# An FNet mixing and SoLU kernel: w_out loaded whole behind x, the first weight product moved into the first transform, copies of turned u shared between two engines, the second pair's sums two steps later

## Chip, cores and metric

The kernel runs on one core of a Trainium2 chip. The metric is device time in microseconds (us) of one execution; each kernel was run several times and medians are given. Engine names are those of the profile: PE multiplies matrices (PEld is its weight load), DVE is the vector engine, ACT the scalar engine, POOL is GpSimd, SP issues most transfers. A profile covers one execution; its span is 1.8 us shorter than the time that the same execution reports (1212.1 against 1213.89 before).

## The reference, cut to what matters

```python
x: (8, 3136, 256)
X = fft(fft(x, axis=1), axis=2).real            # FNet mixing, 3136 = 49 * 64
h = X.reshape(25088, 256) @ w_in                 # w_in (256, 1024)
e = exp(h - max(h)); sm = e / (sum(e) + 1e-9)
solu = h * sm
ln = (solu - mean(solu)) / sqrt(var(solu) + 1e-6) * g_ln
out = ln @ w_out                                 # w_out (1024, 256)
```

w_in and w_out arrive as 64-bit floats. The kernel computes in 32 bits, so it narrows them on DVE, mostly with integer operations, a piece of 512 columns at a time ("narrowing", about 4.5 us a piece).

## The kernel before

The batches go in four pairs. For each pair a first transform (matmuls with the table F, eight chunks) makes z and stores it to memory (`zd`); a gather (`turn`) reads it back turned, as g; a second transform (table T) gives q. Then come units, 25 for a pair and 100 in all; unit 0 of a pair has one sign, the others two. For a unit PE multiplies q with the folded weight Wi (`up`), DVE makes `even`, `join` (with the maximum), and later `product`; ACT does the exponentials and squares; the result u is turned and, four units later, multiplied with Wo (`down`). While a pair's units run, the next pair is loaded, summed with its mirror image, folded and transformed. The first four units' u are turned on PE (`turn_whole`), all later ones by DVE and transfers.

The parts that the change touches, with cuts marked by `# ...`:

```python
def fold_features(o, i):
    # ... two tensor_tensor on DVE
    nc.scalar.copy(o[:, :, 0:129:128], i[:, :, 0:129:128])     # the edge columns

def turn_whole(t):
    # ...
    for s in t.signs:
        for half in range(2):
            # ... four PE turns into a PSUM tile ps
            nc.scalar.copy(uT[:, half * n : (half + 1) * n, :, s], ps)

def centre(self):      # Wo -= its column mean
    # ... 8 matmuls with ones into cs
    nc.scalar.mul(out=wbar, in_=cs, mul=1.0 / FF)
    nc.vector.tensor_tensor(out=Wo, in0=Wo, in1=wbar..., op=ALU.subtract)

def ahead(pr, step):          # the next pair: chunk c summed at step 2+2c, folded one later
    c, r = divmod(step - 2, 2)
    # ...
        if r == 0: add_mirror(pr, c, nc.gpsimd)
        else:      fold(pr, c) # ...

# the opening
weights.piece_in(0)
load(first, 0)
nc.sync.dma_start(out=F, in_=f_tab)
for c in range(1, 4):
    weights.piece_in(c)
    load(first, c, rooms.get(c))
for c in range(4, 6):
    load(first, c, rooms[c])
weights.load_tables()
# ...
for c in range(NC):
    if c < 4:
        weights.narrow_in(c)
    add_mirror(first, c, nc.vector)
    fold(first, c)
    # ...
    elif c == 3:
        weights.place_out()
        weights.load_out(0)
        # ...
    for s in range(CH // 2):
        transform1(first, c * CH // 2 + s)
weights.load_out(1)
turn(first, 0)
weights.place_table()
for h in range(3):
    weights.product_in(h)
for i in range(KF * D // NW):
    weights.narrow_out(i)

# a step of the main loop
even(cur, up(cur, 0)); odd = up(cur, 1)
# ... second transform of the unit after next; its q copied by ACT
turn_whole(prv)            # only units 0 to 3
join(cur, odd)
expo(cur)
ahead_pe(ahd, cur.k1)      # first-transform matmuls of the next pair
ps_o = [down(old, s) for s in old.signs]
product(cur, s)            # each sign
square(cur, s)             # each sign
# ...
stats(cur)
if i == 0:
    weights.centre()
```

Of the kernel before, what the change touches and what calls it, by code (L numbers as in the profile page):

```python
# [20 lines left out]
NK = N1 // 2 + 1  # L21
NH = N2 // 2
PR = 2 * N1
ZR = 4 * NK
CH = 4
NC = NH // CH

KG = 5
# [6 lines left out]
def kernel(  # L35
# [19 lines left out]
    nc = tc.nc  # L55
# [59 lines left out]
            nc.sync.dma_start(out=x0, in_=x_pn[r, 0:1, :])  # L115
        pr.raw[c] = (xa, xb, x0)

    def fold_features(o, i):
        up, down = i[:, :, 1:128], i[:, :, 255:128:-1]
        nc.vector.tensor_tensor(out=o[:, :, 1:128], in0=up, in1=down, op=ALU.add)  # L120
        nc.vector.tensor_tensor(out=o[:, :, 129:256], in0=up, in1=down, op=ALU.subtract)
        nc.scalar.copy(o[:, :, 0:129:128], i[:, :, 0:129:128])  # L122

    def add_mirror(pr, c, engine):

# [6 lines left out]
    def fold(pr, c):  # L132

        xa, _, x0 = pr.raw.pop(c)
        y = xpool.tile([PR, CH, D], FP32, tag="y", name="y")
        fold_features(y, xa)
        pr.y[c] = y
        if c == NC - 1:
            pr.y0 = xpool.tile([PR, 1, D], FP32, tag="y0", name="y0", bufs=1)
            fold_features(pr.y0, x0)  # L140

    def transform1(pr, s):

# [28 lines left out]
    def turn(pr, i):  # L172

        pr.g[i] = gpool.tile([P, KG, D], FP32, tag="g", name="g")
        for j in range(4):
            k = j * NK + i * KG
            nc.gpsimd.dma_start(out=pr.g[i][j * NH : (j + 1) * NH, :, :],  # L177
                                in_=pr.zd[k : k + KG, :, :].rearrange("k n d -> n k d"))
# [58 lines left out]
    def expo(t):  # L237
        t.esum = small.tile([P, 2], FP32, tag="esum", name="esum")
        for s in t.signs:
            t.u[s] = fpool.tile([P, FF], FP32, tag="u", name="u", bufs=2)  # L240
            nc.scalar.activation(out=t.u[s], in_=t.h[s], func=ACT.Exp, bias=t.neg[:, s : s + 1],  # L241
                                 accum_out=t.esum[:, s : s + 1])
# [45 lines left out]
    def turn_whole(t):  # L288

        uT = t.batch.uT[:, t.w].rearrange("p c i (n s) -> p c (i n) s", s=2)  # L290
        n = KF // 2
        for s in t.signs:
            for half in range(2):
                ps = ps_m.tile([P, n, P], FP32, tag="m", name="ps_t")
                for c in range(n):
                    f = half * n + c
                    nc.tensor.matmul(ps[:, c, :], t.u[s][:, f * P : (f + 1) * P], ident, is_transpose=True,
                                     start=(c == 0), stop=(c == n - 1), skip_group_check=True)
                nc.scalar.copy(uT[:, half * n : (half + 1) * n, :, s], ps)

    def move_blocks(batch, units, engines=(nc.sync,)):

# [152 lines left out]



    def ahead(pr, step):

        c, r = divmod(step - 2, 2)  # L460
        if step == 0:
            load(pr, 0)
            load(pr, 1)
        elif 0 <= c < NC:
            if r == 0:
                add_mirror(pr, c, nc.gpsimd)
            else:
                fold(pr, c)
                if c + 2 < NC:
                    load(pr, c + 2)  # L470

    def ahead_pe(pr, step):

        if 0 <= step - 4 < NH // 2:
            transform1(pr, step - 4)
        elif step - 4 >= NH // 2:
            turn(pr, step - 4 - NH // 2)

    with tc.manual_schedule():
        pairs = [Pair(p) for p in range(NP)]  # L480
# [4 lines left out]
        rooms = {}  # L485
# [2 lines left out]
            room = room[0:PR].rearrange("p w c i m -> p (w c i m)").rearrange("p (a n) -> p a n", a=4)  # L488
            rooms[c], rooms[c + 1] = [room[:, i] for i in (0, 1)], [room[:, i] for i in (2, 3)]
        weights.load_in()  # L490
        weights.piece_in(0)
        load(first, 0)
        nc.sync.dma_start(out=F, in_=f_tab)
        for c in range(1, 4):
            weights.piece_in(c)
            load(first, c, rooms.get(c))
        for c in range(4, 6):
            load(first, c, rooms[c])
        weights.load_tables()
        nc.vector.memset(ones, 1.0)  # L500
        nc.vector.memset(neg_half, -0.5)
        bits(top_bit, neg_half[:, 0:1].bitcast(I32), 31, ALU.logical_shift_right, 31, ALU.logical_shift_left)
        nc.vector.memset(T, 0.0)
        for c in range(NC):
            if c < 4:
                weights.narrow_in(c)
            add_mirror(first, c, nc.vector)
            fold(first, c)
            if c + 6 < NC:
                load(first, c + 6)  # L510
            if c == 1:
                weights.load_table()
            elif c == 3:
                weights.place_out()
                weights.load_out(0)
                weights.mid()
                weights.scale_out()
            for s in range(CH // 2):
                transform1(first, c * CH // 2 + s)
        weights.load_out(1)  # L520
        turn(first, 0)
        weights.place_table()
        for h in range(3):
            weights.product_in(h)
        for i in range(KF * D // NW):
            weights.narrow_out(i)
# [7 lines left out]
        for i in range(len(units) + lag):  # L534
# [18 lines left out]
                turn_whole(prv)  # L553
            if cur:
                join(cur, odd)
                expo(cur)
            if ahd:
                ahead_pe(ahd, cur.k1)
# [2 lines left out]
            if cur:  # L561
                for s in cur.signs:
                    product(cur, s)
                for s in cur.signs:
                    square(cur, s)
                    if i >= whole:
                        turn_blocks(cur, s)
            if old:
                scale(old, 0, ps_o[0])
            if cur:  # L570
# [2 lines left out]
                elif cur.w and i >= whole:  # L573
                    move_blocks(batch, slice(0, 2))
                stats(cur)
            if i == 0:
                weights.centre()
            if 0 < i + 1 < NK // KG:
                turn(first, i + 1)
            if ahd:  # L580
# [80 lines left out]
```

## Time and profile before

| what | before | where it is read |
|---|---|---|
| time, median | 1215.85 us (1213.6 to 1216.08, 3 runs) | runs |
| time of the profiled execution | 1213.89 us | runs |
| span | 1212.1 us | page |
| second transform starts | 72.25 us | PE in order of time |
| even of unit 0 starts | 78.91 us | DVE in order of time |
| PE's last wait ends | 118.50 us | PE's waits and its order of time |
| span less that moment | 1093.6 us | worked out |

PE is busy 96% of the span, and after 118.50 us it never waits again. The prediction below shows the lines that this reading rests on. What it calls "the lock" is the 2.3 us by which DVE's product of unit 3 is longer beside POOL's sum: 3.51 us, against 1.22 without it. In a profile line xN counts instructions: a matmul of the program that is not a turn stands there as two (the 8 of `centre` as x16).

### The profile page before, as it was taken

How to read it: one execution, taken by the hardware profiler on the slowest of the kernel's cores; microseconds unless marked ns; L12 is line 12 of the kernel's file. 1: busy time of each engine (PE TensorE's matmuls, PEld its weight loads, DVE VectorE, ACT ScalarE, POOL GpSimd, SP SyncE). 2: the span in 40 equal slices, each digit the busy share in tenths (PEclk: the TensorE clock that was granted, in tenths of full speed). 3: DMA queues.
4: the chain of work that ended last, by engine and by line, in shares of the span. 5: the costliest groups of instructions: out<-in, count | busy, mean ns of one | idle time of the engine just before them, and what ended most of it. 6: DMA issues, size and time to landing. Idle time of an engine off the chain costs nothing. (4 is left out here: it accounts for less than half of the span.)

```text
span 1212.1 us, 15808 instructions
## 1 busy us (share of the span) xinstructions
PE 1166.4 (96%) x4720; PEld 881.5 (73%) x4720; DVE 903.2 (75%) x1240; ACT 644.8 (53%) x1301; POOL 544.0 (45%) x966
## 2 busy tenths in 40 slices
PE   2787999999999999999999999999999999999998
PEld 1444777777777777777777777777777777777787
DVE  7857877777777877777777887777686787778770
ACT  1237655655555565565554555556555555555551
POOL 3027545444554555543453555544463333333333
PEclk9998999999999999999999999999999999999999
DMA  9733688976999888867899889887899587775765
GB/s 237 209 99 104 130 173 159 171 146 127 179 177 171 155 187 167 165 146 136 163 186 189 147 174 168 168 160 141 155 167 163 103 134 124 124 136 102 135 112 114
DMA packets 457382, 184.98 MB, mean 153 GB/s; under 512 B 425510, under 2 KB 439086, under 8 KB 457296
## 3 DMA queue, kind: packets, MB, share of 16 engines
q1 hardware_dynamic: 443216, 144.89, 68.1%
q0 software_dynamic: 14080, 39.08, 12.5%
q8 instruction: 38, 0.62, 0.2%
q14 instruction: 48, 0.39, 0.1%
HBM read 44.37 MB, written 38.80 MB: 69 GB/s over the span
## 5 line engine op out<-in xcount | busy, mean ns | idle before, releaser
L314 PE MATMUL ps_o<-Wo,uT 128*128 128x256 f32 x3136 | 693.2, 379 | 0.0
L314 PEld LDWEIGHTS ps_o<-Wo,uT 128*128 128x128 f32 x3136 | 611.8, 196 | 61.7 <-issue 1.0
L216 PE MATMUL ps_h<-Wi,q 128*128 128x512 f32 x800 | 364.5, 599 | 2.4 <-DVE ev L222 2.4
L249 DVE SCALAR_TENSOR_TENSOR u<-h,u 128x1024 f32<-128x1024 f32 x196 | 234.8, 1235 | 158.2 <-ACT u L241 105.4
L258 ACT ACTIVATE h<-u,nmean 128x1024 f32<-128x1024 f32 x196 | 223.6, 1141 | 126.3 <-POOL nmean L251 126.3
L251 POOL TENSOR_SCALAR nmean<-usum 128x1 f32<-128x1 f32 x196 | 127.2, 650 | 357.3 <-DVE u L249 356.9
L230 DVE CUSTOM_DVE_ANT_0 h<-ev,ps_h 128x1024 f32<-128x1024 f32 x196 | 231.7, 1219 | 45.0 <-PE ps_h L216 40.3
L216 PEld LDWEIGHTS ps_h<-Wi,q 128*128 128x128 f32 x800 | 153.4, 192 | 153.7 <-issue 146.2
L286 DVE STREAM_TRANSPOSE v<-u 128x1024 f32<-128x1024 f32 x192 | 227.9, 1227 | 0.1
L241 ACT ACTIVATE u<-h,neg 128x1024 f32<-128x1024 f32 x196 | 223.6, 1141 | 3.3
L222 DVE SCALAR_TENSOR_TENSOR ev<-w_mid,r,ps_h 128x1024 f32<-128x1024 f32 x100 | 127.6, 1276 | 51.8 <-PE ps_h L216 47.2
L194 ACT COPY q<-ps 128x256 f32<-128x256 f32 x100 | 37.2, 372 | 178.9 <-PE ps L188 175.7
L326 POOL DMA_INDIRECT out_dram<-ot,idx x96 | 102.8, 1071 | 33.3 <-issue 18.7
L235 ACT ACTIVATE neg<-nmax 128x2 f32<-128x2 f32 (+1 forms) x100 | 20.4, 204 | 176.1 <-DVE nmax L230 176.1
L165 PE MATMUL ps<-y,F 98*100 98x258 f32 (+3 forms) x288 | 81.4, 423 | 28.8 <-DVE y L120 26.5
L270 POOL TENSOR_SCALAR v<-ssq 128x2 f32<-128x2 f32 (+1 forms) x100 | 26.2, 262 | 167.2 <-ACT h L258 166.2
L319 ACT ACTIVATE ot<-ps_o,rs 128x256 f32<-128x256 f32 x196 | 83.3, 458 | 25.3 <-DMA out_dram<-ot,idx 12.8
L188 PEld LDWEIGHTS ps<-T,g 128*128 128x128 f32 x400 | 60.1, 191 | 50.0 <-issue 48.1
L165 PEld LDWEIGHTS ps<-y,F 98*100 98x100 f32 x288 | 50.2, 196 | 45.3 <-ACT y L122 34.0
L273 POOL TENSOR_TENSOR rs<-v,neg_half 128x2 f32<-128x2 f32 (+1 forms) x100 | 72.5, 725 | 7.8
L177 POOL DMA_DIRECT2D g<-zd x80 | 47.7, 608 | 49.9 <-DMA zd<-z_u 41.7
L188 PE MATMUL ps<-T,g 128*128 128x128 f32 x400 | 60.7, 275 | 2.3 <-DMA g<-zd 2.3
(65 smaller groups left out, 466.5 us busy)
## 6 DMA issues: line engine op xcount, KB each, us to landing
uT<-v SPq DMA_DIRECT2D x752, 128.0 KB
g<-zd POOLq DMA_DIRECT2D x80, 160.0 KB, 5.3
out_dram<-ot SPq DMA_DIRECT2D x100, 128.0 KB
zd<-z SPq DMA_DIRECT2D x28, 400.0 KB
xa<-in_x_dram SPq DMA_DIRECT2D x28, 392.0 KB
raw_in<-in_moe_w_in_dram SPq DMA_DIRECT2D x4, 512.0 KB
raw_out<-in_moe_w_out_dram SPq DMA_DIRECT2D x2, 1024.0 KB
zd<-z_u SPq DMA_DIRECT2D x4, 400.0 KB
```

The source lines that it names most:

```text
L165: nc.tensor.matmul(o[..., cs], F[:, 2 * t + h, :], i[..., cs], start=first, stop=True, skip_group_check=True)
L188: nc.tensor.matmul(ps[:, h * P : (h + 1) * P], g[:, k, h * P : (h + 1) * P], T[:, k1, :], start=(h == 0), stop=True, skip_group_check=True)
L216: nc.tensor.matmul(ps[:, fs], t.q[:, c * P : (c + 1) * P], Wi[:, c, fs], start=True, stop=True)
L222: nc.vector.scalar_tensor_tensor(out=t.ev, in0=w_mid, scalar=t.r, in1=ps, op0=ALU.mult, op1=ALU.add)
L230: nc.vector.tensor_tensor_reduce(out=t.h[s], in0=t.ev, in1=ps, scale=1.0, scalar=-3.0e38, op0=ALU.subtract if s else ALU.add, op1=ALU.max, ...
L241: nc.scalar.activation(out=t.u[s], in_=t.h[s], func=ACT.Exp, bias=t.neg[:, s : s + 1], accum_out=t.esum[:, s : s + 1])
L249: nc.vector.scalar_tensor_tensor(out=t.u[s], in0=t.h[s], scalar=1.0, in1=t.u[s], op0=ALU.mult, op1=ALU.mult, accum_out=t.usum[:, s : s + 1])
L251: nc.gpsimd.tensor_scalar(out=t.nmean[:, s : s + 1], in0=t.usum[:, s : s + 1], scalar1=-1.0 / FF, scalar2=None, op0=ALU.mult)
L258: nc.scalar.activation(out=t.h[s], in_=t.u[s], func=ACT.Square, bias=t.nmean[:, s : s + 1], accum_out=t.ssq[:, s : s + 1])
L286: nc.vector.transpose(out=t.batch.v[:, t.w, :, o], in_=t.u[s])
L314: nc.tensor.matmul(ps, uT[:, c, :, s], Wo[:, c, :], start=(c == 0), stop=(c == KF - 1))
L326: dma = nc.gpsimd.indirect_dma_start(out=out, out_offset=bass.IndirectOffsetOnAxis(ap=idx[:, i : i + 1], axis=0), in_=t.ot[s], in_offset=None)
```

## The change

The intent is to let units start sooner and to shorten the first few of them. It has four parts: (1) the opening: the first two pieces of w_in are loaded and narrowed first, the Q table comes ahead of two x chunks, both halves of w_out are asked for together in the middle of the first transform, the first w_in product is made there too, and DVE copies the edge columns for the first pair; (2) the centring of Wo goes ahead of unit 0's squares; (3) two of the four copies of turned u go from ACT to DVE; (4) the second pair's sums start at step 4 instead of 2 and catch up later.

```diff
-        nc.scalar.copy(o[:, :, 0:129:128], i[:, :, 0:129:128])
+        copy(o[:, :, 0:129:128], i[:, :, 0:129:128])
 ...
+        copy = nc.scalar.copy if pr.p else nc.vector.tensor_copy
 ...  (turn_whole)
-                nc.scalar.copy(uT[:, half * n : (half + 1) * n, :, s], ps)
+                if s:
+                    t.wait.append((uT[:, half * n : (half + 1) * n, :, s], ps))
+                else:
+                    nc.scalar.copy(uT[:, half * n : (half + 1) * n, :, s], ps)
 ...  (ahead, ahead_pe follow this table)
+    START = [[2 + 2 * c for c in range(NC)], [4, 6, 8, 10, 12, 13, 15, 16]]
 ...  (opening)
-        weights.piece_in(0)
-        load(first, 0)
-        nc.sync.dma_start(out=F, in_=f_tab)
-        for c in range(1, 4):
+        for c in range(4):
             weights.piece_in(c)
-            load(first, c, rooms.get(c))
+            if c:
+                load(first, c - 1, rooms.get(c - 1))
+            if c == 1:
+                nc.sync.dma_start(out=F, in_=f_tab)
+        load(first, 3, rooms[3])
+        weights.load_tables()
         for c in range(4, 6):
             load(first, c, rooms[c])
-        weights.load_tables()
 ...
-            if c < 4:
-                weights.narrow_in(c)
+            if c < 3:
+                for i in ((0, 1), (2,), (3,))[c]:
+                    weights.narrow_in(i)
 ...
-                weights.load_out(0)
+                for i in range(2):
+                    weights.load_out(i)
 ...
-        weights.load_out(1)
+            if c == 3:
+                weights.product_in(0)
         turn(first, 0)
         weights.place_table()
-        for h in range(3):
+        for h in range(1, 3):
             weights.product_in(h)
 ...  (main loop)
+            if prv:
+                for o, ps in prv.wait:
+                    nc.vector.tensor_copy(out=o, in_=ps)
+            if cur:
                 expo(cur)
 ...
                     product(cur, s)
+                if i == 0:
+                    weights.centre()
                 for s in cur.signs:
                     square(cur, s)
 ...
-            if i == 0:
-                weights.centre()
```

More of the change, by code (lines that the diff above doesn't have):

```diff
@@ L116, in load, with fold_features @@
         pr.raw[c] = (xa, xb, x0)
-    def fold_features(o, i):
+    def fold_features(o, i, copy):
         up, down = i[:, :, 1:128], i[:, :, 255:128:-1]
@@ L135, in fold @@
         y = xpool.tile([PR, CH, D], FP32, tag="y", name="y")
-        fold_features(y, xa)
+        copy = nc.scalar.copy if pr.p else nc.vector.tensor_copy
+        fold_features(y, xa, copy)
         pr.y[c] = y
@@ L139, in fold @@
             pr.y0 = xpool.tile([PR, 1, D], FP32, tag="y0", name="y0", bufs=1)
-            fold_features(pr.y0, x0)
+            fold_features(pr.y0, x0, copy)
     def transform1(pr, s):
@@ L291, in turn_whole @@
         n = KF // 2
+        t.wait = []
         for s in t.signs:
@@ L454, in centre @@
             nc.vector.tensor_tensor(out=Wo, in0=Wo, in1=wbar.unsqueeze(1).to_broadcast([P, KF, D]), op=ALU.subtract)
+    START = [[2 + 2 * c for c in range(NC)], [4, 6, 8, 10, 12, 13, 15, 16]]
     def ahead(pr, step):
-        c, r = divmod(step - 2, 2)
+        start = START[pr.p == 1]
         if step == 0:
@@ L463, in ahead @@
             load(pr, 1)
-        elif 0 <= c < NC:
-            if r == 0:
+        for c in range(NC):
+            if step == start[c]:
                 add_mirror(pr, c, nc.gpsimd)
-            else:
+            if step == start[c] + 1:
                 fold(pr, c)
@@ L472, in ahead_pe @@
     def ahead_pe(pr, step):
-        if 0 <= step - 4 < NH // 2:
-            transform1(pr, step - 4)
-        elif step - 4 >= NH // 2:
-            turn(pr, step - 4 - NH // 2)
+        for c in range(NC):
+            for half in range(2):
+                if step == START[pr.p == 1][c] + 2 + half:
+                    transform1(pr, c * CH // 2 + half)
+        if 0 <= step - 20 < NK // KG:
+            turn(pr, step - 20)
     with tc.manual_schedule():
```

## The prediction

> **What bounds the kernel now.** I read the page first (busy shares, then the row of slices), then PE's waits after the opening, then the time-ordered views of PE, DVE, ACT and POOL over the first 130 us.
>
> ```profile
> PE 1166.4 (96%) x4720; PEld 881.5 (73%) x4720; DVE 903.2 (75%) x1240; ACT 644.8 (53%) x1301; POOL 544.0 (45%) x966
> PE   2787999999999999999999999999999999999998
> ```
>
> PE is busy 96%, and what it lacks is in the first four slices of 30.3 us. All waits of PE from 112 us to the end are these two:
>
> ```profile
> PE ps_t L297 <- ACT q L194: 2.2, 1, 2.2
> PE ps_t L297 <- DVE u L249: 0.8, 1, 0.8
> ```
>
> So from some moment on PE never waits, and its list of work is fixed. The end is that moment plus a constant; a change to the opening is worth what it moves that moment by, and nothing else. PE in order of time (start, duration, group, then the idle time before it):
>
> ```profile
> 54.78 4.59 PE L165 MATMUL ps<-y,F 98*100 98x258 f32 x16 [0.79 <-ACT y L122]
> ...
> 72.25 1.13 PE L188 MATMUL ps<-T,g 128*128 128x128 f32 x8 [2.32 <-DMA g<-zd]
> 73.40 5.39 PE L216 MATMUL ps_h<-Wi,q 128*128 128x512 f32 x8
> ...
> 118.50 0.66 PE L297 MATMUL ps_t<-ident,u 128*128 128x128 f32 x4 [2.19 <-ACT q L194]
> ```
>
> The moment is 118.50 us: the last PE turn of unit 3, for which ACT first had to free a PSUM buffer (the q copy behind unit 3's squares). What leads there is DVE:
>
> ```profile
> 51.94 0.43 DVE L352 TENSOR_SCALAR tmp<-raw_out 128x512 int32<-128x512 int32 x1 [0.67 <-DMA raw_out<-in_moe_w_out_dram]
> ...
> 69.81 0.43 DVE L352 TENSOR_SCALAR tmp<-raw_out 128x512 int32<-128x512 int32 x1 [8.68 <-DMA raw_out<-in_moe_w_out_dram]
> ...
> 78.91 1.27 DVE L222 SCALAR_TENSOR_TENSOR ev<-w_mid,r,ps_h 128x1024 f32<-128x1024 f32 x1
> ...
> 86.27 2.29 DVE L454 TENSOR_TENSOR Wo<-Wo,wbar 128x2048 f32<-128x2048 f32 x1 [1.93 <-ACT wbar L453]
> ...
> 110.93 3.51 DVE L249 SCALAR_TENSOR_TENSOR u<-h,u 128x1024 f32<-128x1024 f32 x1 [2.41 <-ACT u L241]
> ```
>
> It waits 8.68 us for the second half of w_out, narrows it until 79, and only then can the first unit's even part start (78.91). The other even parts start at 88.48, 96.11, 104.68 and 116.72: steps of 9.57, 7.63, 8.57 and 12.04 us. The last is long for a reason to be seen on POOL and ACT:
>
> ```profile
> 110.98 2.37 POOL L129 TENSOR_TENSOR xa<-xa,xb 98x1020 f32<-98x1020 f32 x1
> 113.30 1.21 POOL L130 TENSOR_TENSOR xa<-xa,xb 98x4 f32<-98x4 f32 x1
> 114.55 1.72 POOL L251 TENSOR_SCALAR nmean<-usum 128x1 f32<-128x1 f32 x2
> ```
> ```profile
> 98.84 2.14 ACT L299 COPY uT<-ps_t 128x512 f32<-128x512 f32 x4
> 100.86 0.21 ACT L235 ACTIVATE neg<-nmax 128x2 f32<-128x2 f32 x1
> ```
>
> POOL's mirror sum for the second pair runs beside DVE's product, which takes 3.51 instead of 1.22 us. And ACT's four copies of turned u stand in front of neg, though DVE had the maxima at 99.95.
>
> [...] 3.51 against 1.22 us, over by 2.3, about the 2.37 of the POOL sum. [...] a first-transform chunk takes 3.70 us for 8 matmuls, against 1.03 for 4 later on, and the first up product takes 5.39 against 3.60[...]. [...] half a w_out, issued at 39.12, was usable at 51.94, 12.8 us on[...]. [...]
>
> **Part 1, the loads and the first transform.** Now two w_in pieces are narrowed before the first sums: this fills DVE's 3.13 us wait for x, and narrowing takes 4.4 us each (16.23 to 20.66). So the first sums start near 10.65 + 4.4 = 15.05 instead of 13.78; each sum and fold takes 2.45, now plus about 0.15 for the edge copy, which leaves ACT (the column there costs 98x4 0.16 us). Chunks 0, 1, 2 reach PE at about 17.8, 24.7, 31.7 (were 15.82, 22.74, 29.70), and chunk 3, without a piece before it, at 34.3 (was 36.55). Q comes ahead of x's chunks 4 and 5, so instead of 38.6 by roughly 35. PE then does chunk 3 (to 38), the first w_in product (3.6 warm, say 4.8 with a cold start, to 43), and runs without gaps[...]: chunks 4 to 7 of about 2.1 us each, the last bound by DVE and two y buffers, end near 52 instead of 59.4. The 0.8 us gaps behind ACT's edge copies go.
>
> The last z is therefore ready about 7 us sooner, but it can't land so much sooner. By 50 us the windows add up to 11.75 MB. By the last z's landing about 14.7 MB must have passed: eight x chunks twice (6.3), w_in 2.1, w_out 2.1, z 3.2, tables about 1. The rest, 2.9 MB at the 265 GB/s that windows around 50 us show, takes 11 us: 61, with the tail of a landing 62 to 62.5 (was 65.1, where POOL began its turn issues at 65.16). Before, g was used 7.1 us after that, while w_out's second half was being moved too (0.8 to 0.96 share, 62 to 70 us). Now it isn't, so 6 to 7: PE starts the second transform at about 68.5 (was 72.25), and up, cold again after the gap (5.39), ends at about 75.
>
> On DVE, w_out's first half is there at about 52.5 and its second, 1.05 MB later, about 56. Four narrowings of 4.6 us run without a gap, 52.5 to 71. Up's first half is there at 68.5 + 1.1 + 2.7 = 72.3: unit 0's even starts there, its join at 75 (was 80.34). **Gain so far about 5.3 us**, though the wait removed was 8.68: the z and g chain takes over.
>
> **Part 2, the centring** moves ahead of the squares. PE's 16 column sums end at 75 + 0.6 + 3.6 = 79.2; ACT's wbar follows at once (to 79.7) and no longer waits behind a square; the 2.29 us subtraction ends at 82, where even of unit 1 starts (was 88.48). **Gain 6.5 us in all.** Step 1 to 2 is unchanged (7.63; unit 0 has one sign).
>
> **Part 3, shared copies.** In each of the steps 2, 3, 4 two of ACT's four copies (1.05 us) go to DVE, after the join. ACT: squares end 2.47 after even's start, q, two copies, neg at +3.97 instead of +4.75. DVE's two copies[...] fit in its 2.4 us wait for exp. **0.8 us a step, 1.6 in two**: step 7.8.
>
> **Part 4, the sums two steps later.** Step 3 to 4 loses the lock (2.3) and the fold in front of the even part (0.69 + 0.67, 1.2 from start to start): 12.04 - 8.57 = **3.5 us**. The same work then falls into steps where PE has seven microseconds of down products per step (7.07) and waits for none of it.
>
> Even of unit 4: 82 + 7.63 + 7.8 + 7.8 = 105.2 (was 116.72, so 11.5 sooner). In the step before, the even part was held back by the fold, after the squares' delay; now squares of unit 3 and q end 2.83 after even, where they ended 1.73 after it (118.45 - 116.72). So the gain at PE's last wait is 11.5 - 1.1 = 10.4, and the moment is about 108. From there PE's total is the same: the first-transform products missing in steps 4 and 5 are done in 15 and 18.
>
> **Rivals.** (a) DMA takes it all back: w_out's second megabyte goes ahead of z3 to z7[...]. For: DMA share 0.9 to 1.1 up to 46 us. Against: 0.65 to 0.03 from 48 to 60 us. If the last z still lands at 65, up's cold second half ends at 78.8 and parts 2 to 4 give 5 to 6: about 1210. (b) Second-pair sums and folds now crowd steps 12 to 17, and steps 13, 14 and 16 have both. A DVE step with fold is 11.1 (126.66 to 137.74), with the lock 2.3 more, 13.4 against PE's 11.65; two in a row lag 3.5 us. For: DVE is nearly at PE's pace. Against: even frees its PSUM half at 127.9 and PE refills it at 135.09, 7.2 us of slack. If it stalls PE: plus 2 to 4, 1208 to 1210. (c) DVE's PSUM copies are late and hold back the product: loses 1.6, 1207. (d) POOL's descriptors for g are held up by DVE's narrowing, now beside them[...]: plus 1 to 3. In the other direction, g may come within 5 us and the chain be DVE's narrowing: 1 to 2 us less.
>
> **Range and chances.** 1215.85 - 10.4 = 1205.4; as the rivals cost more than the upside gives, 1205.8. The upper end is rival (a) or (b) at its worst; the lower end is the quicker g (2 us), a quicker landing of the last z (1 to 2) and the run-to-run spread (1213.6 to 1216.1). Faster by 2% needs 24 us; PE's waits between its first matmul and 118.5 us add up to 24.8 (the idle times of its view in order of time), and most of them stay. Slower by 2% has no mechanism here.
>
> **What would show it.** PE's last wait near 108 instead of 118.5 and none after; no DVE wait for w_out between its halves, narrowing ended near 71; last z landed near 62, second transform near 68.5; first even near 72; evens of units 1 to 4 near 82, 90, 97.5, 105; product of unit 3 at 1.2 us; chunks 4 to 7 at about 2 us on PE. The prediction is wrong if PE waits again after 120 us (b), if the second transform starts after 71 (a, d), or if steps 2 to 4 keep 8.6 us (c).

## The result, and the profile after

The changed kernel took 1202.73 us (median of 5, 1202.06 to 1203.28). The kernel before took 1215.85 in the same rounds (5 runs, 1213.6 to 1216.71). The ratio is 0.9894, with a 95% interval of 0.988 to 0.9909. A ratio here is the mean time of one kernel's runs over that of the other's of the same rounds, so it is not quite the ratio of the medians. The change is faster by 1.1%, which is within 2%. The prediction was 1205.8 with a range of 1201 to 1210.5.

The page of the changed kernel, PE's busy share and its row of 40 slices (30.0 us each):

```profile
PE 1155.5 (96%) x4720; PEld 877.0 (73%) x4720; DVE 905.8 (75%) x1255; ACT 640.4 (53%) x1286; POOL 543.8 (45%) x966
PE   2868999999999999999999999999999999999998
```

From the fifth digit on the row is as before. The first four digits sum to 24 in both rows: PE's early work is placed otherwise (a fuller second and fourth slice, an emptier third), and the row, in tenths, is too coarse to show what was gained. All waits of PE from 105 us to the end (total, times, longest):

```profile
PE ps_t L299 <- ACT q L195: 1.8, 1, 1.8
```

There is one, and it is of the same kind as the last one before. PE in order of time (start, duration, group, idle time before it):

```profile
41.47 5.39 PE L166 MATMUL ps<-y,F 98*100 98x258 f32 x24
...
47.66 2.42 PE L166 MATMUL ps<-y,F 98*100 98x258 f32 x16 [0.79 <-ACT z_u L169]
...
68.25 2.05 PE L189 MATMUL ps<-T,g 128*128 128x128 f32 x8 [11.30 <-DMA g<-zd]
70.08 4.58 PE L217 MATMUL ps_h<-Wi,q 128*128 128x512 f32 x8
...
107.12 0.66 PE L299 MATMUL ps_t<-ident,u 128*128 128x128 f32 x4 [1.84 <-ACT q L195]
```

The moment went from 118.50 to 107.12 us, by 11.38. The span less the moment is 1200.8 - 107.12 = 1093.7, against 1093.6 before. Note also the 11.30 us that PE idles for g ahead of the second transform: before, PE made all three w_in products there and idled 2.32. PE is slower after it: the second transform's 8 matmuls take 2.05 us instead of 1.13. The profile also gives the clock that PE is granted, as a share of full speed; read in slices of 0.2 us it is 0.50 from 61.8 to 72.1 us here. "Half clock" and "cold" mean this below, "warm" the full clock.

DVE in order of time:

```profile
51.10 0.43 DVE L357 TENSOR_SCALAR tmp<-raw_out 128x512 int32<-128x512 int32 x1 [3.53 <-DMA raw_out<-in_moe_w_out_dram]
...
73.04 1.28 DVE L223 SCALAR_TENSOR_TENSOR ev<-w_mid,r,ps_h 128x1024 f32<-128x1024 f32 x1 [3.52 <-PE ps_h L217]
...
79.02 2.29 DVE L459 TENSOR_TENSOR Wo<-Wo,wbar 128x2048 f32<-128x2048 f32 x1 [0.31 <-ACT wbar L458]
...
100.31 1.33 DVE L573 COPY uT<-ps_t 128x512 f32<-128x512 f32 x2
101.94 1.23 DVE L250 SCALAR_TENSOR_TENSOR u<-h,u 128x1024 f32<-128x1024 f32 x1 [0.30 <-ACT u L242]
```

The wait between the two halves of w_out is gone; narrowing runs through and ends near 69.5, and now DVE waits 3.52 us for PE's up product before the first even part. The centring sits close behind the product. The two copies take 1.33 us and fit where DVE waited 2.4 us for the exponentials. Unit 3's product takes 1.23 instead of 3.51 us.

POOL shows where the mirror sum went, and when the last z was usable (the 38.74 us are POOL's own idle time):

```profile
63.02 2.48 POOL L178 DMA_DIRECT2D g<-zd  x4 [38.74 <-DMA zd<-z_u]
...
115.87 2.35 POOL L129 TENSOR_TENSOR xa<-xa,xb 98x1020 f32<-98x1020 f32 x1
```

ACT now has two copies in front of neg, of 1.14 us, instead of four of 2.14; and during the first transform it waits for a z buffer, which will matter later:

```profile
56.20 1.07 ACT L169 COPY z_u<-ps 100x512 f32<-100x512 f32 x2 [6.57 <-DMA zd<-z_u]
...
91.59 1.14 ACT L304 COPY uT<-ps_t 128x512 f32<-128x512 f32 x2
92.74 0.20 ACT L236 ACTIVATE neg<-nmax 128x2 f32<-128x2 f32 x1
```

Where the 11.38 us come from, by DVE's even parts (evens of units 0 to 4 start at 73.04, 81.23, 88.86, 96.55 and 104.24; before at 78.91, 88.48, 96.11, 104.68 and 116.72):

| stretch | before | after | gain |
|---|---|---|---|
| start to even of unit 0 | 78.91 | 73.04 | 5.87 |
| even 0 to even 1 (centring, and cold up product) | 9.57 | 8.19 | 1.38 |
| even 1 to even 2 | 7.63 | 7.63 | 0 |
| even 2 to even 3 (shared copies) | 8.57 | 7.69 | 0.88 |
| even 3 to even 4 (shared copies, later sums) | 12.04 | 7.69 | 4.35 |
| even 4 to PE's last wait | 1.78 | 2.88 | -1.10 |
| sum | 118.50 | 107.12 | 11.38 |

### The profile page after: what moved, and what is told of

The parts are those of the page before. It is cut to its first block, busy times and chain, and to the rows that moved or that the text cites. A ratio compares the mean times of both kernels' runs of the same rounds, so it can differ in the third digit from the quotient of the medians.

```text
span 1200.8 us, 15804 instructions
## 1 busy us (share of the span) xinstructions
PE 1155.5 (96%) x4720; PEld 877.0 (73%) x4720; DVE 905.8 (75%) x1255; ACT 640.4 (53%) x1286; POOL 543.8 (45%) x966
## 3 DMA queue, kind: packets, MB, share of 16 engines
q1 hardware_dynamic: 443216, 144.89, 68.5%
## 5 line engine op out<-in xcount | busy, mean ns | idle before, releaser
L319 PEld LDWEIGHTS ps_o<-Wo,uT 128*128 128x128 f32 x3136 | 611.6, 196 | 61.8 <-issue 1.0
L166 PE MATMUL ps<-y,F 98*100 98x258 f32 (+3 forms) x288 | 72.7, 390 | 24.6 <-DVE y L122 23.8
L166 PEld LDWEIGHTS ps<-y,F 98*100 98x100 f32 x288 | 46.3, 179 | 37.0 <-DVE y L122 21.3
L189 PE MATMUL ps<-T,g 128*128 128x128 f32 x400 | 61.6, 278 | 11.3 <-DMA g<-zd 11.3
```

The source lines that it names most:

```text
L166: nc.tensor.matmul(o[..., cs], F[:, 2 * t + h, :], i[..., cs], start=first, stop=True, skip_group_check=True)
L189: nc.tensor.matmul(ps[:, h * P : (h + 1) * P], g[:, k, h * P : (h + 1) * P], T[:, k1, :], start=(h == 0), stop=True, skip_group_check=True)
L319: nc.tensor.matmul(ps, uT[:, c, :, s], Wo[:, c, :], start=(c == 0), stop=(c == KF - 1))
```

## The experiments

The theory was that the time is a constant plus the end of PE's last wait, so that every part is worth what it moves that moment by. The rival was that some parts give nothing (their time would be lost elsewhere), or that the later part of the kernel takes some of it back. Except where said otherwise, experiments start from the changed kernel. In the results "moment" is the end of PE's last wait on a turn (`ps_t`) in the experiment's profile; times are medians. The kernel before ran beside them with medians from 1214.3 to 1215.33, and all twelve gave correct outputs. The changed kernel itself was not run again beside them: "over" and "under" it compare medians of different rounds, and the experiments ran on three chips. The kernel before took 1209.45 to 1216.71 us in single runs of all rounds. The ratios compare within rounds, and by them the experiments come out up to 2 us slower against the changed kernel than by the medians. So a difference of less than 2 us in time decides nothing here, and the readings rest on the moments and the chains before them.

| kernel | time | ratio to before | second transform | even 0 | moment | span less moment | first down products |
|---|---|---|---|---|---|---|---|
| before | 1215.85 | | 72.25 | 78.91 | 118.50 | 1093.6 | 3.62 |
| after | 1202.73 | 0.9894 | 68.25 | 73.04 | 107.12 | 1093.7 | 3.73 |
| undo_centre | 1206.03 | 0.993 | 69.15 | 73.49 | 109.17 | 1093.6 | 3.73 |
| undo_share | 1206.65 | 0.9929 | 69.67 | 74.00 | 109.83 | 1095.8 | 5.10 |
| undo_later | 1208.29 | 0.9946 | 69.77 | 74.63 | 111.93 | 1093.6 | 3.62 |
| no_opening | 1209.59 | 0.9964 | 72.60 | 79.48 | 114.92 | 1093.8 | 3.73 |
| out1_last | 1202.28 | 0.9897 | 68.24 | 75.15 | 109.69 | 1093.6 | 3.73 |
| undo_mid | 1201.77 | 0.9902 | 69.04 | 73.49 | 107.56 | 1093.6 | 3.73 |
| undo_edge | 1203.28 | 0.9913 | 68.56 | 74.11 | 108.30 | 1093.9 | 3.73 |
| wout_alone | 1209.79 | 0.9967 | 70.40 | 74.03 | 113.84 | 1095.3 | 5.23 |
| wout_and_later | 1203.99 | 0.9905 | 70.12 | 73.74 | 107.80 | 1095.8 | 5.41 |
| warm | 1204.72 | 0.9918 | 68.82 | 71.98 | 106.04 | 1097.3 | 5.42 |
| split_z | 1199.45 | 0.9879 | 65.01 | 70.56 | 104.72 | 1093.7 | 3.73 |
| split_turn_tab | 1196.94 | 0.9863 | 62.60 | 67.22 | 101.28 | 1093.6 | 3.73 |

In 10 of the 14 profiles the span less the moment is 1093.6 to 1093.9, although the moment itself ranges over 17 us. In the other four (1095.3 to 1097.3) the first 16 down products of the last column take 5.1 to 5.4 us instead of 3.6 to 3.7. That is PE beginning the unbroken stretch at half clock, and costs 1.4 to 1.7 us: in windows of 2 us the granted clock went down to 0.52 there in undo_share, 0.50 in wout_alone and 0.50 in warm; in wout_and_later it is taken from the 5.41 us alone. Three of the four also have a later wait of PE, of 0.2, 0.3 and 1.3 us; up to 0.6 us more are not accounted for. More of this under "warm".

### undo_centre: the centring back behind the squares

```diff
                     product(cur, s)
-                if i == 0:
-                    weights.centre()
 ...
                 stats(cur)
+            if i == 0:
+                weights.centre()
```

> The changed kernel with the centring back behind the squares and statistics of the first unit, all else kept. My theory: every microsecond before PE's last wait counts fully. ACT then does the square (1.3 us) before wbar, so the subtraction starts at about 80.8 instead of 79.02, unit 1's even part at about 83.1 instead of 81.23, PE's last wait ends at about 109.0 instead of 107.12, and the time is 1202.7 + 1.9 = 1204.6. Rival: the later chain has room and absorbs it, then the last wait stays at 107 and the time within 0.5 us of 1202.7.

Measured: 1206.03 us (1204.55 to 1206.84), ratio to before 0.993 (0.9917 to 0.9944), so 3.3 us over the changed kernel by the medians. In the profile the moment is 2.05 us later. DVE of this kernel in order of time:

```profile
81.08 2.29 DVE L459 TENSOR_TENSOR Wo<-Wo,wbar 128x2048 f32<-128x2048 f32 x1 [1.93 <-ACT wbar L458]
```

DVE waits 1.93 us for wbar again (the same as before the change) where the changed kernel waits 0.31. The step from even 0 to even 1 is 9.80 instead of 8.19: 1.61 us for this part. The rest of the 2.05 is a first even 0.45 us later. The opening is the same in both kernels. First evens of the four kernels with an unaltered opening lie between 73.04 and 74.63, and the last z is usable at 63.02 to 64.47 in these profiles. So up to 1.6 us at the moment can come from the transfers of one execution and not from the edit.

### undo_share: all copies of turned u back on ACT

```diff
-                if s:
+                if False:
                     t.wait.append((uT[:, half * n : (half + 1) * n, :, s], ps))
```

> The changed kernel with all copies of turned u on ACT again. My theory: steps between even parts grow from 7.69 to about 8.57 us for two steps, PE's last wait ends at about 108.9 instead of 107.12, time about 1204.4. Rival: DVE is the fuller engine there, so giving it the copies only moved the load; then undoing costs nothing or gains, and the steps stay at 7.7.

Measured: 1206.65 us (1205.11 to 1207.37), ratio 0.9929 (0.9916 to 0.9943), 3.9 over the changed kernel; the moment is 2.71 us later. ACT, then DVE, of this kernel in order of time:

```profile
101.11 2.15 ACT L304 COPY uT<-ps_t 128x512 f32<-128x512 f32 x4
```
```profile
104.65 1.22 DVE L250 SCALAR_TENSOR_TENSOR u<-h,u 128x1024 f32<-128x1024 f32 x1 [2.43 <-ACT u L242]
```

The four copies stand in front of neg again and DVE waits 2.43 us for the exponentials where the changed kernel waits 0.30 behind its own copies. The steps from even 2 on are 8.57 instead of 7.69: 0.88 us each, 1.76 in two; the first even was 0.96 later. The profiled execution also began the unbroken stretch cold (5.10), which is in its span and not in its moment.

### undo_later: the second pair's sums at steps 2, 4, ... again

```diff
-    START = [[2 + 2 * c for c in range(NC)], [4, 6, 8, 10, 12, 13, 15, 16]]
+    START = [[2 + 2 * c for c in range(NC)]] * 2
```

> The changed kernel with the second pair's sums at the steps of the other pairs (2, 4, ... 16). My theory: the sum of POOL runs beside unit 3's second product again, which takes about 3.4 us instead of 1.22, and a fold stands before unit 4's even part: PE's last wait ends 2.4 to 3.5 us later, at about 110, time about 1205.5. Rival: moving the sums crowds steps 12 to 17 and takes as much back there; then undoing them costs less than 1 us.

Measured: 1208.29 us (1206.45 to 1209.1), ratio 0.9946 (0.9932 to 0.9959), 5.6 over the changed kernel: the dearest single part. DVE, then POOL:

```profile
103.51 4.37 DVE L250 SCALAR_TENSOR_TENSOR u<-h,u 128x1024 f32<-128x1024 f32 x1 [0.29 <-ACT u L242]
```
```profile
104.43 2.35 POOL L129 TENSOR_TENSOR xa<-xa,xb 98x1020 f32<-98x1020 f32 x1
106.74 1.20 POOL L130 TENSOR_TENSOR xa<-xa,xb 98x4 f32<-98x4 f32 x1
```

The product of unit 3 takes 4.37 us instead of 1.23. It began 0.92 us ahead of POOL's first sum and yet stands until 107.88, which is 1.1 us after that sum ended: it was held for the whole of it. Why a product that began first is held is not shown. POOL's second sum, of one column, then takes 1.20 us beside the product, and 0.20 in the changed kernel. The step from even 3 to even 4 is 12.03, as in the kernel before (12.04), against 7.69: 4.34, less the 1.10 of the last row of the table above, is 3.24 us for this part. The first even was 1.59 later here, and 3.24 + 1.59 = 4.83 is the 4.81 by which the moment moved.

So parts 2 to 4 are worth 1.6, 1.8 and 3.2 us at the moment, without what the first even varied by.

### no_opening: the whole of part 1 undone

The diff is the opening of the change, backwards: old order of loads and narrowing, w_out's second half asked for after the last z, all three products after the transform, edge copies on ACT. Parts 2 to 4 stay.

> The changed kernel without any of its opening part: loads, narrowing order, w_in product and edge copies as before; centring, shared copies and later sums kept. My theory: these three are worth 1.9 + 1.6 + 2.4 to 3.5, about 6 to 7 us, so PE's last wait ends at about 112 and the time is about 1209.5; the opening is worth the other 6 to 7. Rival: the parts are not additive, the later three hide behind the opening or the other way round, and this lands within 2 us of one of the two kernels.

Measured: 1209.59 us (1207.5 to 1210.48), ratio 0.9964 (0.9947 to 0.998): 6.9 over the changed kernel. The first even is at 79.48, 6.44 later, as in the kernel before (78.91). The moment is 7.80 later; the remaining 1.36 us come from the steps. So the time came as expected and the moment 2.9 us later than the 112 expected (the profiled execution was the slowest of the six, 1210.48 us), and the reason was a surprise. POOL of this kernel:

```profile
85.01 2.20 POOL L252 TENSOR_SCALAR nmean<-usum 128x1 f32<-128x1 f32 x1 [17.57 <-DVE u L250]
```

nmean works on one column, takes 0.25 us in the changed kernel and 2.20 here. wbar was ready just as the product ended, so the subtraction of 2.29 us on DVE began ahead of POOL's small operation. The squares wait for nmean and are late, and two units later a join (DVE, 1.22 us long, at 97.23) waits 1.26 us for a buffer that they hold; the step is 8.73 instead of 7.69. The next step is 8.60: PE's up product there takes 6.15 us, where the next one takes 3.60. In the changed kernel nmean starts at 78.81 and the subtraction at 79.02: part 2 escapes this by 0.2 us. The parts therefore don't add up: undone one by one they come to 7.80 + 1.6 + 1.8 + 3.2 = 14.4 us at the moment, while the change as a whole gave 11.38.

### out1_last: w_out's second half asked for last, the rest of the change kept

```diff
-                for i in range(2):
-                    weights.load_out(i)
+                weights.load_out(0)
 ...
+        weights.load_out(1)
         turn(first, 0)
```

> The changed kernel with only the load of w_out's second half put back behind the last z. My theory: the early load no longer gains anything in the changed kernel, because z3 to z7 queue behind it (ACT waits 6.57 us for a z buffer, PE then idles 11.3 us). Put back, the last z lands 4 to 5 us sooner (near 58 instead of 63), w_out's second half still comes by about 61, the second transform starts near 64.5 instead of 68.25, unit 0's even part near 70 instead of 73.04; PE's last wait ends near 104 and the time is 1199.5 to 1200.5, below the changed kernel. Rival, the change's intent: narrowing waits for the second half again, up to 8.7 us, and the time rises to 1206 or more.

Measured: 1202.28 us, no different from the changed kernel, but with a wide scatter (1199.4 to 1205.71); ratio 0.9897 (0.9878 to 0.9915). I had expected a gain of 2 to 3 us and the rival a loss of 3 or more, so both miss. DVE waits for the half again, though for less. DVE and POOL:

```profile
66.03 0.43 DVE L357 TENSOR_SCALAR tmp<-raw_out 128x512 int32<-128x512 int32 x1 [3.57 <-DMA raw_out<-in_moe_w_out_dram]
```
```profile
80.68 2.20 POOL L252 TENSOR_SCALAR nmean<-usum 128x1 f32<-128x1 f32 x1 [16.36 <-DVE u L250]
```

The wait is 3.57 instead of 8.68 us. Since the transform ends sooner on PE with the rest of the opening, the late load is itself issued at 56.3 instead of 60.35. POOL begins its issues for g at 61.89, only 1.1 us sooner than in the changed kernel where 4 to 5 were expected; beside the late load g then takes 6.35 us instead of 5.23, and the second transform starts at 68.24, as in the changed kernel. The first even, at 75.15, no longer waits for PE: DVE goes to it straight from narrowing. In the profile the moment is 2.57 later than in the changed kernel, of which 2.11 are the first even and 1.05 the late nmean again, less 0.64 in the step before it; the median of the runs doesn't show it. The profiled execution took 1205.05 and the fastest of the five 1199.4. Why it scatters so is open.

### undo_mid and undo_edge: the first product back behind the transform; the edge copies back on ACT

```diff
-            if c == 3:
-                weights.product_in(0)
 ...
-        for h in range(1, 3):
+        for h in range(3):
             weights.product_in(h)
```

> The changed kernel with the first w_in product back behind the whole first transform. My theory: nothing is lost, since PE idles 11.3 us before the second transform and that wait is set by the last z's landing: time 1202.7 within 1 us; PE's idle before the second transform shrinks by about what the product takes. Rival, the intent: the product in the middle shortens the path to the first up product[...]; undoing it then costs 2 us or more[...].

```diff
-        copy = nc.scalar.copy if pr.p else nc.vector.tensor_copy
+        copy = nc.scalar.copy
```

> The changed kernel with the first pair's edge columns copied by ACT again. My theory: PE's gaps in chunks 4 to 7 come back (ACT's copy stands behind a z copy that waits), the transform ends 1 to 3 us later on PE, but the last z still lands near 63 because its buffer and the queue set it: time 1202.7 within 1 us. Rival: the gaps are on the path, time 1204.5 or more.

Measured: 1201.77 us (1201.1 to 1202.95; 0.9902, 0.9885 to 0.992) and 1203.28 us (1202.26 to 1203.96; 0.9913, 0.9897 to 0.9929), 1.0 under and 0.5 over the changed kernel by the medians, 1.0 and 2.3 over it by the ratios, whose intervals overlap: neither is worth anything that can be told from the scatter. PE of undo_mid:

```profile
69.04 2.05 PE L189 MATMUL ps<-T,g 128*128 128x128 f32 x8 [4.10 <-DMA g<-zd]
```

Before the second transform PE idles 4.10 us for g instead of 11.30, and still idles. The time of the product or of the 0.8 us gaps on PE was taken out of a stretch in which PE has time to spare, as z and g are what is waited for. In undo_edge the idle time is 6.9 us. Its moment is 1.18 later, of which the first even is 1.07: there up took 5.45 us instead of 4.58. A first even of 74.11 lies within the 73.04 to 74.63 above.

### wout_alone: the kernel before, with only w_out's second half asked for early

```diff
                 weights.load_out(0)
+                weights.load_out(1)
 ...
-        weights.load_out(1)
         turn(first, 0)
```

> The kernel before with only the load of w_out's second half moved up behind the first. My theory: the 8.68 us wait of DVE goes, but the last z was ready only at 60 us and lands at about 64 to 65, the second transform starts at about 71 to 72, and up's cold second half sets the first join near 78 instead of 80.3: gain 2 to 3 us, time about 1213. Rival: the wait was the bound, and its removal gains nearly 8 us, 1207.5.

Measured: 1209.79 us (1209.16 to 1210.93), ratio 0.9967 (0.9952 to 0.9983). That is 4.5 us under the median of before in the same rounds (1214.3); the moment went from 118.50 to 113.84, by 4.66. I had expected 2 to 3, the rival 8. One line moved brings the first even part 4.88 us forward, of the 5.87 of the whole change. PE of this kernel:

```profile
71.94 3.70 PE L216 MATMUL ps_h<-Wi,q 128*128 128x512 f32 x8 [0.49 <-ACT q L194]
...
113.84 0.66 PE L297 MATMUL ps_t<-ident,u 128*128 128x128 f32 x4 [2.19 <-ACT q L194]
115.38 5.23 PE L314 MATMUL ps_o<-Wo,uT 128*128 128x256 f32 x16
```

It gives more than expected for two reasons. The second transform starts at 70.40 where 71 to 72 was expected, as g comes without a load beside it, at most 5.4 us after the last z (7.1 in the kernel before). And PE makes its three w_in products right up to the second transform, with no idle time, and the up product takes 3.70 us; the kernel before idled 2.32 us there and took 5.39. The first even starts at 74.03, only 1 us behind the changed kernel, although the last z is usable 2 us later (64.97 against 63.02). The last line shows the half-clock beginning of the stretch (granted clock 0.50 from 116 to 118 us).

### wout_and_later: no_opening with both halves of w_out asked for early

This is the early load plus parts 2 to 4.

> The changed kernel without the rest of its opening: the order of the x and w_in loads, the narrowing order, the place of the first w_in product and the edge copies as before; only w_out's early load, the centring, the shared copies and the later sums kept. My theory: w_out's early load alone gives nearly all that the opening gives. Unit 0's even part comes near 74.0 as in the run with that load alone, then the changed kernel's own steps (8.2, 7.6, 7.7, 7.7) lead to 105.2 for unit 4 and PE's last wait near 108, time 1203 to 1204. Rival: the two first narrowings before the sums, the earlier table and the product in the middle carry several microseconds themselves: 1206 or more.

Measured: 1203.99 us (1201.58 to 1206.27), ratio 0.9905 (0.9889 to 0.9921). The moment is at 107.80, 0.68 behind the changed kernel. So of all of part 1, the early load carries nearly everything; the rest, with its reordered loads, narrowing, early product and edge copies, gives 1.3 us by the medians and 0.68 at the moment, both within the scatter. Yet out1_last showed that with the rest kept, the early load is hardly missed: no loss in the median, 2.57 us at the moment. The two halves of the opening stand in for each other in good part: by the medians the early load is worth 5.6 us without the rest (no_opening against this kernel), and the rest 7.3 without the early load (no_opening against out1_last). They do so by different paths. With the early load alone the 8.68 us wait is gone and PE's w_in products run straight into the second transform (no idle time before 70.12). With the rest alone the wait shrinks to 3.57 us and DVE's narrowing still sets the first even. Only with both do z and g lead. Which piece of the rest carries it when it stands alone was not run.

### split_z: z stored in 96 and 4 partitions

Where the prediction said that "the z and g chain takes over", the profile allows a check. Not all of the DMA engines were busy while z was being stored. A stretch of two microseconds of the changed kernel (window, then its length, then PE, PEld, DVE, ACT and POOL busy, then granted clock, share of the DMA engines busy, and GB/s):

```profile
52.00:54.00 2.00, 2.00 (x6) 0.95 (x5) 1.90 (x4) 0.00 (x0) 0.00 (x0) 1.00 0.62 241
```

The share is 0.62 to 0.69 from 48 to 60 us. Times 16 engines that is an estimate of 10 to 11 at work at a time, and the trace has 10 packets under way at once there (median). z has 100 partitions. I expected a store of 96 of them, with the other 4 apart, to put more engines to work. The run tests this one cut; why the number of partitions should matter is not shown.

```diff
-            nc.sync.dma_start(out=pr.zd[:, c * CH : (c + 1) * CH, :], in_=pr.z)
+            for r in (slice(0, 96), slice(96, ZR)) if pr.p == 0 else (slice(0, ZR),):
+                nc.sync.dma_start(out=pr.zd[r, c * CH : (c + 1) * CH, :], in_=pr.z[r])
```

> The changed kernel with each store of the first pair's z cut into 96 and 4 partitions. My theory: what sets the changed kernel's second transform is the last z's landing, and the z stores, 100 partitions each, use only 10 of the 16 DMA engines (DMA share 0.62 to 0.69 from 48 to 60 us, where little else moves). Cut so, the share in that stretch rises toward 1, the last z lands 2 to 3 us sooner (near 60.5 instead of 63.0), the second transform starts near 65.7 instead of 68.25, unit 0's even part near 70.5 instead of 73.04, PE's last wait ends near 104.6 instead of 107.12, time near 1200. Rival: the total rate of memory sets the landing, not the number of engines; then nothing moves, 1202.7 within 0.7.

Measured: 1199.45 us (1197.82 to 1200.15, 4 runs), ratio 0.9879 (0.9857 to 0.99), 3.3 under the changed kernel by the medians and 1.8 by the ratios, whose intervals overlap. On the same chip and nearly the same rounds, its slowest run lies below the fastest of the eleven of undo_mid and undo_edge (1201.1). The same window of this kernel:

```profile
52.00:54.00 2.00, 2.00 (x6) 0.83 (x5) 1.90 (x5) 0.00 (x0) 0.00 (x0) 1.00 0.95 381
```

The share is 0.95 and 381 GB/s move instead of 241. The last z is usable at 59.61 instead of 63.02, g at 65.01 instead of 68.25, and the moment is at 104.72, 2.40 sooner. The last z was usable at 63.02 or later in every profile with uncut stores but out1_last (61.89), so this is clear of their scatter. The chain of z and g is shown to be what bounds the opening after the change.

### split_turn_tab: in addition the first gather on SP, and the T table behind w_out

```diff
-        turn(first, 0)
+        turn(first, 0, nc.sync)
 ...
-            if c == 1:
-                weights.load_table()
-            elif c == 3:
+            if c == 3:
                 weights.place_out()
                 # ... both load_out
+                weights.load_table()
```

> The cut z stores, and also the first gather of g issued by SP instead of POOL and the twiddle table loaded behind w_out instead of before it. My theory: the chain from last z to second transform, 5.2 us, loses about 1.5 us (four issues of 0.3 instead of 0.6 us, a quicker start), w_out's first half lands about 1.5 us sooner (50 instead of 51.1), so narrowing ends near 68 instead of 69.5. Second transform near 64, unit 0's even part near 69, PE's last wait near 103, time near 1198.5. Rival: as one of the two chains (DMA to g, or DVE's narrowing) gives way the other holds, and it ends with split_z's 1200 or, if the later table holds back a z store, above it.

Measured: 1196.94 us (1196.64 to 1197.27, 4 runs), ratio 0.9863 (0.9843 to 0.9884). This is the best kernel; it beats both. PE of this kernel:

```profile
62.60 2.05 PE L190 MATMUL ps<-T,g 128*128 128x128 f32 x8 [6.61 <-DMA g<-zd]
...
101.28 0.66 PE L300 MATMUL ps_t<-ident,u 128*128 128x128 f32 x4 [1.84 <-ACT q L196]
```

The second transform starts 5.65 us sooner than in the changed kernel and the moment is 5.84 sooner, still with 1093.6 us to the end. PE still idles 6.61 us for g. The two additions were not run apart, so which of them gave the 2.5 us over split_z is open. In the two profiles most of the gain lies ahead of the gather: the last z store is issued at 54.12 instead of 56.01 and the gather begins at 57.58 instead of 59.61, while from there to the second transform it takes 5.02 instead of 5.40 us.

### warm: filler products before the second transform

```diff
             weights.product_in(h)
+        fill = ps_m.tile([P, 512], FP32, tag="m", name="fill")
+        for _ in range(12):
+            nc.tensor.matmul(fill, ident, weights.w_in[0][:, 0:512], start=True, stop=True)
```

> The changed kernel with twelve needless products of 512 columns on PE in its 11.3 us gap before the second transform. My theory: the half clock after that gap costs about 1.6 us on the path (second transform's 8 matmuls 2.05 instead of 1.13 us, up 4.58 instead of 3.60). With the array kept busy these two go to 1.1 and 3.6, unit 0's even part comes near 71.4 instead of 73.04, PE's last wait ends near 105.6, time near 1201.2. Rival: the clock there is hidden, as DVE and the centring set unit 1's start; then the last wait stays at 107 and the time at 1202.7.

Measured: 1204.72 us (1201.98 to 1205.07), ratio 0.9918 (0.99 to 0.9936): no gain, 2.0 slower by the medians. PE of this kernel:

```profile
69.89 3.70 PE L217 MATMUL ps_h<-Wi,q 128*128 128x512 f32 x8
...
106.04 0.66 PE L299 MATMUL ps_t<-ident,u 128*128 128x128 f32 x4 [1.84 <-ACT q L195]
106.58 5.42 PE L319 MATMUL ps_o<-Wo,uT 128*128 128x256 f32 x16
```

The filler did what it was for: the up product takes 3.70 instead of 4.58 us, and the moment is at 106.04, 1.08 sooner. But after the last wait the down products took 5.42 instead of 3.73, and PE waited once more, 1.3 us, for a turned u. In the profile this is the clock. Two microseconds after the last wait, of this kernel and then of the changed one (the third number from the end is the granted clock):

```profile
108.00:110.00 2.00, 2.00 (x6) 1.64 (x5) 1.66 (x4) 1.65 (x4) 1.58 (x4) 0.50 0.70 205
```
```profile
108.00:110.00 2.00, 2.00 (x11) 1.83 (x10) 1.68 (x5) 1.96 (x5) 2.00 (x5) 1.00 0.26 56
```

The last wait, 1.84 us, is as long as in the changed kernel, where the products after it took 3.73 us. In no_opening and undo_centre, too, a last wait of 1.84 us stands before products of 3.73 us, and in wout_and_later before products of 5.41. So the length of this wait does not decide it, and what makes the clock fall is not shown here. Read in slices of 0.2 us, the granted clock changes at 73.42, 76.84, 90.49, 93.90, 107.56 and 110.97 in the kernel before and at 61.81, 72.05, 92.54 and 95.95 in the changed one: the distances in each are multiples of about 3.41 us. Ahead of its first change the profile gives 1.00 even where a chunk takes 3.70 us.

Two of the six runs took 1202.0 and four 1204.6 to 1205.1; the profiled one is of the slower group. The gain in the moment was real, and the half-clock start with the wait behind it ate it in the profile. That it is the clock in the unprofiled runs too is argued, not shown: the mean granted clock that each run lists doesn't follow its time (before ran 1213.59 and 1216.06 us, both at 0.995).

## Why the prediction was right

The frame held. PE's last wait was predicted "near 108" and came at 107.12, with none after, and the constant behind it was the same within 0.1 us.

The terms, in the prediction's own steps:

| step | predicted | measured |
|---|---|---|
| chunks 0, 1, 2 on PE | 17.8, 24.7, 31.7 | 17.42, 24.31, 31.23 |
| last z usable | 62 to 62.5 | 63.02 |
| g after that | 6 to 7 us | 5.23 us |
| second transform | 68.5 | 68.25 |
| narrowing ends | near 71 | about 69.5 |
| even of unit 0 | 72.3 | 73.04 |
| even of unit 1 | 82 | 81.23 |
| steps 1-2, 2-3, 3-4 | 7.63, 7.8, 7.8 | 7.63, 7.69, 7.69 |
| even 4 to the moment | 2.83 | 2.88 |
| moment | about 108 | 107.12 |

**Part 1.** "Gain so far about 5.3 us, though the wait removed was 8.68: the z and g chain takes over" was right in mechanism (split_z shows it) and in size: the 5.3 are those of the join, predicted at 75 and measured at 74.70 (80.34 before, so 5.64). The close hit on the second transform is in part luck: z was usable 0.5 to 1.0 us later than predicted, and g followed it 0.8 to 1.8 us sooner. Nor was the last z "ready about 7 us sooner": its copy ended at 57.27 against 60.00, 2.7 us sooner, because ACT waited 6.57 us for a z buffer. And the 265 GB/s from which the landing was worked out was no fixed limit, as split_z moved 381. What the prediction did not see is that most of its pieces are not needed. Its working gives each reordering its own place in the sum; undo_mid and undo_edge show that product and edge copies give nothing at the end, wout_alone that a single moved load gives 4.66 us of the moment.

**The mis-sized terms.** The first even was put at 72.3 and came at 73.04. The sum gave the second transform 1.1 us, as if warm, and put all of the cold on up (5.39); the cold came earlier, so that the transform took 2.05 and up 4.58. The even of unit 1 was put at 82 and came at 81.23, and that is most of the 0.9 us by which the moment was missed. It doesn't depend on the first even but on PE's column sums and wbar. There the cold made little difference (2.05 + 4.58 = 6.63 against 1.1 + 5.39 = 6.49). The transform started 0.25 sooner, and the sum added whole durations where the groups of PE overlap by 0.16 to 0.22 us each: the column sums ended at 78.57 and not at 79.2. wbar took 0.45 us from there where 0.5 was allowed.

**Parts 3 and 4** were right to about 0.1 us each: the steps are 7.69 where 7.8 was predicted, and DVE's two copies took 1.28 to 1.33 us, within its wait of 2.41 before. For part 4, "loses the lock (2.3) and the fold in front of the even part (...1.2...)" gives 3.5; undoing it in the changed kernel costs 4.34 at the step. The product is held longer there: with the exponentials no longer late it begins 0.92 us ahead of POOL's first sum instead of 0.05, and is held until that sum ends both times, so it takes 4.37 us instead of 3.51.

**The rivals.** (a) is false, the last z came 2 us sooner. (b) is false, PE never waits after 107. (c) is false, the steps took 7.69. (d) was not seen: POOL's issues for g took 2.48 us, against 2.42 before.

**The subtraction at the end.** 10.4 us were taken from 1215.85. The moment moved by 11.4, and the measured gain is 13.1 by the medians, 11.3 between the two profiled executions. The other 1.8 are that the profiled execution of before took 1213.89, below its median, while the profiled one of after, 1202.6, is at its median. Some executions begin the unbroken stretch at half clock, worth 1.7 us between profiles, which would be of this size; that it is the cause of the scatter of before is not shown. This puts the measurement nearer to the lower end of the range than to the middle.

## What to carry to other kernels

When one engine is saturated from a certain moment on, measure every change by that moment and not by the waits it removes: here 8.68 us of wait were worth 5.9, and in ten of fourteen profiles the moment gave the span to 0.3 us; in the other four PE began cold there. Parts of an opening can stand in for each other, so undo them singly and together before giving each its share: singly two of them showed nothing and a third no clear loss in time, all together 6.9 us (7.8 at the moment). And look for what the removed wait uncovers: here it was stores of 100 partitions at a DMA share of 0.62 to 0.69, and cutting them in 96 and 4 (0.95 from 52 to 54 us) gave another 2.4 us at the moment, 3.3 by the medians.
